# Moving one gate load of the second chunk from the head of the input transfers to behind the seventh weight piece

## The chip, the cores and the metric

The kernel runs on one core of a Trainium2 chip. The metric is the time of one execution in microseconds on the device, and the median over several executions is what two versions are compared by. The engines named below are TensorE (PE, its weight loads PEld), VectorE (DVE), ScalarE (ACT), GpSimd (POOL) and SyncE (SP), which computes nothing here and only issues transfers.

## The reference

Two layers follow each other. The first is a gated linear attention over 4 batches, 8 heads, 768 steps and a head dimension of 48:

```
f = 1.0 / (1.0 + np.exp(-f_logit))
for t in range(S):
    state = f[:, :, t, :, None] * state + np.einsum('bhd,bhe->bhde', k[:, :, t], v[:, :, t])
    y[:, :, t] = np.einsum('bhd,bhde->bhe', q[:, :, t], state)
```

Its output, 3072 rows of 384 (8 heads times 48), goes through four dense experts of width 1024, whose outputs are added with the normalized weights of each row:

```
p = domain_probs / (domain_probs.sum(-1, keepdims=True) + 1e-09)
for e in range(E):
    h = np.maximum(x @ w1[e], 0.0)
    out += p[:, e:e + 1] * (h @ w2[e])
```

All tensors come and go as 32-bit floats. The matrix products run in bf16.

## The kernel before, in words

The 768 steps are cut into 6 chunks of 128. Inside a chunk the recurrence becomes matrix products. For each batch the gate logits `f` go through an exponential (line 260) and a logarithm (264) on ACT, a triangular product on TensorE sums them along the steps (268), two exponentials of the sums (288) scale `q` and `k` (296), both are transposed (305 on TensorE in the first chunks, 309 by DMA later), and then come the masked products (320, 324), the output (331, 335), the state (341, 348, 355), and the transposed output `xT` (360 on TensorE, 313 by DMA), which the experts read. The four batches of a chunk make 512 rows. For them the first expert layer takes 24 matmuls per expert (364: 8 blocks of 128 columns, 3 blocks of the inner dimension), its results pass the relu on ACT (375) or DVE (373), and the second layer (379) takes 32 matmuls, whose results are weighted and added on DVE (386) or ACT (388).

Chunk 0 must run its attention before any expert work can start. From there on the attention of the next chunk runs beside the expert work of the current one. While TensorE waits in chunk 0, idle matmuls on a tile `busy` (614) keep it occupied; the planner says how many.

The weights of the experts are loaded once, by DMAs that GpSimd issues (239) and that cast to bf16. There are 11 pieces, numbered from 0: pieces 0 and 1 are the two halves of the first layer of expert 0, 2 and 3 those of expert 1, 4 and 5 the halves of the second layer of expert 0, then whole layers follow: 6 is the first layer of expert 2, 7 the second of expert 1, 8 the first of expert 3, 9 the second of expert 2, 10 the second of expert 3. Pieces 0 to 5 write 384 KB each and the rest 768 KB. Piece 0 waits for the last `q` of chunk 0 (line 241), so that the inputs of chunk 0 go first; piece 10 waits for `k` of chunk 1 (243).

The inputs are loaded by DMAs that SyncE issues (232), in the order of its queue. Chunk 0 has one load of 192 KB per tensor and batch. Of chunk 1, the gate logits of batch 0 come next, alone; those of batch 1 wait for piece 8 (`w_gate`), and behind them stand `k`, `q` and `v` of batches 0 and 1 and all of batches 2 and 3, in loads of 384 KB. The first exponential of chunk 1 reads the logits of batches 0 and 1 in one instruction, so it needs both loads. A queue runs in order: a load that waits holds everything behind it on SyncE.

No order is written out by hand. `Plan.run` simulates the engines with a list of operations, each with a cost per engine, a priority and its dependences, and gives out the buffers. Each step takes the ready operation of the lowest priority number, and the kernel emits the instructions in that order. The two halves of a copy or a relu may therefore land on ACT or DVE, depending on the planned times. A load is an operation of the planned engine "DMA"; `cost=0.1` for the moved load is a planned cost, not a measured one. `after(x, y)` makes the DMA x wait on the chip until the DMA y has landed.

Of the kernel before, what the change touches and what calls it, by code (L numbers as in the profile page):

```python
# [102 lines left out]
def kernel(  # L103
# [85 lines left out]
    ins = {}  # L189
# [10 lines left out]
    def tl(kind, *key):  # L200

        if (kind, key) not in tiles:
            room = kind if kind in rooms else "ps_m" if kind in ("hp", "op", "pp") else "ps_t"
            slot = P.slot[(room, kind) + key if room.startswith("ps_") else (room,) + key]
            if room in ("gp", "qk", "e"):
                tiles[kind, key] = pads[room, slot]
            else:
                shape, dt = shapes[kind]
                pool = ps if room.startswith("ps_") else wk
                tiles[kind, key] = pool.tile(shape, dt, name=f"{room}{slot}")  # L210
        return tiles[kind, key]

    def after(later, earlier):
        tc.add_manual_dep(later.ins, earlier.ins.name,
                          mybir.DependencyInfo(mybir.DependencyClass.Sync, mybir.DependencyReason.DATA),
                          reason="order of transfers")
# [4 lines left out]
    def hh(b, n=1):  # L221
        return slice((b % 2) * H, (b % 2 + n) * H)
# [8 lines left out]
    def load(c, nm, b, n):  # L231
        ins[c, nm, b] = nc.sync.dma_start(out=tl(nm, c, b // 2)[:, hh(b, n), :],  # L232
                                          in_=srcs[nm][c, :, b * H:(b + n) * H, :])
        if (c, nm, b) == (1, "f", 1):
            after(ins[c, nm, b], ins["w", w_gate])

    def load_w(i, e, which, ks, cols):
        w, r = (w1_sb, w1_r) if which == 1 else (w2_sb, w2_r)
        ins["w", i] = nc.gpsimd.dma_start(out=w[:, e, ks, cols], in_=r[e][:, ks, cols])  # L239
        if i == 0:  # L240
            after(ins["w", 0], ins[0, "q", B - 1])
        if i == w_last:
            after(ins["w", i], ins[1, "k", 0])
# [154 lines left out]
    def add_load(c, nm, b, n, prio, deps=(), cost=None):  # L398
        op = P.add(f"ld {nm}{c}.{b}", {"DMA": cost or (1.05 if c else 1.1) * n}, lambda e: load(c, nm, b, n), prio,
                   deps=deps, takes=[(nm, c, b // 2)], lag=2.0)  # L400
        for i in range(n):
            ld[c, nm, b + i] = op
        return op

    for i, x in enumerate("f0 k0 q0 f1 k1 q1 f2 f3 k2 q2 v0 k3 q3 v1 v2 v3".split()):
        add_load(0, x[0], int(x[1]), 1, -1000 + i)
    add_load(1, "f", 0, 1, -980, cost=0.1)

    every = slice(0, None)
    pieces = [(e, 1, every, slice(i * F // 2, (i + 1) * F // 2)) for e in range(2) for i in range(2)]  # L410
# [2 lines left out]
    w_last, w_gate = len(pieces) - 1, len(pieces) - 3  # L413
    wd = {}
    for i, (e, which, ks, cols) in enumerate(pieces):
        if i == w_last:
            for x in ((1, "f", 1, 1), (1, "k", 0, 2), (1, "q", 0, 2), (1, "v", 0, 2)):
                add_load(*x, -430 + len(ld), deps=wd[3, 1])
        iss = P.add(f"w issue {i}", {"POOL": 0.8}, lambda _, i=i, x=(e, which, ks, cols): load_w(i, *x),
                    -500 + i, deps=[ld[0, "q", B - 1]] + ([ld[1, "k", 0]] if i == w_last else []))  # L420
        op = P.add(f"w {i}", {"DMA": 2.25 if i < 6 else 4.5}, lambda _: None, -400 if i == w_last else -460 + i, deps=[iss], lag=1.5)
        wd[e, which] = wd.get((e, which), []) + [op]
# [226 lines left out]
```

## Time and profile before

| what | value |
|---|---|
| median of 5 runs | 299.07 us (298.53 to 299.54) |
| the profiled execution | 299.54 us |
| its span, first to last instruction | 297.7 us |
| granted TensorE clock | 1.0 of full speed |
| busy: PE, ACT, DVE, POOL | 287.3, 176.3, 125.8, 106.4 us |
| moved by DMA | 36.82 MB, mean 124 GB/s |

The profiled execution is the slowest of the five shown. Times inside it are counted from the first instruction; the remaining 1.84 us lie around the span. A name such as "PE ps_m L364" means the engine, the tile it writes and the line of the kernel. "SPq" is SyncE's queue, and the length of a row there is the time that the issue took, waits included, not the transfer. The time from an issue to the landing of its data is a number of its own. Some matmul records are missing from the trace, a few per cent, which looks like short gaps.

### The profile page before, as it was taken

How to read it: one execution, taken by the hardware profiler on the slowest of the kernel's cores; microseconds unless marked ns; L12 is line 12 of the kernel's file. 1: busy time of each engine (PE TensorE's matmuls, PEld its weight loads, DVE VectorE, ACT ScalarE, POOL GpSimd, SP SyncE). 2: the span in 40 equal slices, each digit the busy share in tenths (PEclk: the TensorE clock that was granted, in tenths of full speed). 3: DMA queues.
4: the chain of work that ended last, by engine and by line, in shares of the span. 5: the costliest groups of instructions: out<-in, count | busy, mean ns of one | idle time of the engine just before them, and what ended most of it. 6: DMA issues, size and time to landing. Idle time of an engine off the chain costs nothing.

```text
span 297.7 us, 5544 instructions
## 1 busy us (share of the span) xinstructions
PE 287.3 (96%) x2132; PEld 170.6 (57%) x2160; DVE 125.8 (42%) x247; ACT 176.3 (59%) x325; POOL 106.4 (36%) x179
## 2 busy tenths in 40 slices
PE   6969999999999999999999999999999999999995
PEld 2547555567777776455565555555555555555553
DVE  6757002685674583036375444332533322201223
ACT  5866664847675686777465574545465544465440
POOL 5387301329488159235448463234220000000000
PEclk9999999999999999999999999999999999999999
DMA  7999999976979969995989952102432100200003
GB/s 155 214 190 206 207 207 213 203 139 169 185 154 196 210 138 188 201 222 93 208 156 208 186 110 36 29 0 62 115 64 39 26 2 26 79 2 0 0 0 108
DMA packets 136462, 36.82 MB, mean 124 GB/s; under 512 B 126812, under 2 KB 135644, under 8 KB 136436
## 3 DMA queue, kind: packets, MB, share of 16 engines
q1 hardware_dynamic: 129348, 30.14, 50.7%
q0 software_dynamic: 7088, 6.33, 13.6%
q8 instruction: 17, 0.28, 0.4%
q14 instruction: 9, 0.07, 0.1%
HBM read 31.51 MB, written 4.72 MB: 122 GB/s over the span
## 4 chain that ended last, share of the span: by engine, by line
PE 91%; DMA 3%; SPq 3%; issue 1%; DVE 1%
PE ps_m L379 42%; PE ps_m L364 41%; SPq L232 3%; DMA w_sb<-in_moe_w_dram 2%; PE ps_t L320 2%; PE ps_t L335 1%; PE ps_t L331 1%; DMA q<-in_q_dram 1%; PE ps_t L341 1%; PE ps_t L268 1%; PE ps_t L305 0%; SPq L247 0%; DVE h L373 0%; DVE o L386 0%; PE ps_t L360 0%
## 5 line engine op out<-in xcount | busy, mean ns | idle before, releaser
L375 ACT ACTIVATE h<-ps_m 128x512 bf16<-128x512 f32 (+1 forms) x192 | 102.5, 538 | 93.7 <-PE ps_m L364 89.9
L364 PE MATMUL ps_m<-xT,w_sb 128*128 128x512 bf16 (+1 forms) x670 | 150.1, 341 | 3.5 <-DMA w_sb<-in_moe_w_dram 2.0
L379 PE MATMUL ps_m<-w_sb,h 128*128 128x384 bf16 (+1 forms) x776 | 151.6, 324 | 0.2
L379 PEld LDWEIGHTS <-h 128*128 128x128 bf16 x776 | 75.1, 98 | 58.6
L386 DVE SCALAR_TENSOR_TENSOR o<-ps_m,pn,o 128x384 f32<-128x384 f32 (+1 forms) x73 | 44.7, 612 | 110.6 <-PE ps_m L379 104.3
L364 PEld LDWEIGHTS <-w_sb 128*128 128x128 bf16 x696 | 65.5, 98 | 45.1 <-DMA w_sb<-in_moe_w_dram 2.7
L296 POOL TENSOR_TENSOR qk<-q,e 128x384 bf16<-128x384 f32 x19 | 22.9, 1208 | 36.6 <-ACT e L288 34.3
L324 DVE TENSOR_TENSOR AT<-ps_t,mask 128x512 bf16<-128x512 f32 x48 | 29.9, 683 | 5.5 <-PE ps_t L320 5.4
L355 POOL TENSOR_TENSOR Sf<-Sf,egs 48x192 f32<-48x192 f32 x40 | 20.2, 504 | 32.5 <-DVE Sf L348 30.4
L288 ACT ACTIVATE e<-ps_t 128x384 f32<-128x384 f32 x48 | 26.7, 666 | 4.0 <-PE ps_t L268 2.9
L373 DVE TENSOR_SCALAR h<-ps_m 128x256 bf16<-128x256 f32 (+1 forms) x40 | 20.0, 510 | 20.0 <-PE ps_m L364 17.8
L296 POOL TENSOR_TENSOR qk<-k,e 128x384 bf16<-128x384 f32 x20 | 20.4, 1024 | 8.8 <-ACT e L288 4.3
L348 DVE TENSOR_TENSOR Sf<-Sf,ps_t 48x192 f32<-48x192 f32 x40 | 14.0, 351 | 11.0 <-PE ps_t L341 9.7
L239 POOL DMA_DIRECT2D w_sb<-in_moe_w_dram x11 | 9.0, 824 | 20.2 <-DMA k<-in_k_dram 16.6
L356 POOL CAST sb<-Sf 48x192 bf16<-48x192 f32 x40 | 13.6, 340 | 2.6
L388 ACT ACTIVATE o<-ps_m,pn 128x384 f32<-128x384 f32 x22 | 12.8, 581 | 2.8 <-PE ps_m L379 1.8
L293 POOL DMA_DIRECT2D egs<-e x16 | 9.0, 565 | 10.4 <-ACT e L288 10.4
L614 PE MATMUL ps_m<-busy 128*128 128x512 bf16 x32 | 10.5, 427 | 1.6 <-DVE busy L144 1.5
L226 ACT CAST yb<-ps_t 128x384 bf16<-128x384 f32 (+1 forms) x16 | 7.6, 472 | 7.5 <-PE ps_t L335 7.3
L335 PE MATMUL ps_t<-vb,AT 128*128 128x48 bf16 x192 | 11.5, 185 | 0.4 <-DVE vb L228 0.4
L260 ACT ACTIVATE ex<-f 128x768 f32<-128x768 f32 (+1 forms) x14 | 10.5, 748 | 2.1 <-DMA f<-in_f_logit_dram 2.0
L335 PEld LDWEIGHTS <-AT 128*128 128x128 bf16 x192 | 9.9, 97 | 2.1 <-DVE vb L228 0.5
(54 smaller groups left out, 122.5 us busy)
## 6 DMA issues: line engine op xcount, KB each, us to landing
out_dram<-o SPq DMA_DIRECT2D x23, 192.0 KB, 2.0
w_sb<-in_moe_w_dram POOLq DMA_DIRECT2D x5, 768.0 KB, 18.5
k<-in_k_dram SPq DMA_DIRECT2D x10, 384.0 KB, 4.8
q<-in_q_dram SPq DMA_DIRECT2D x10, 384.0 KB, 5.1
v<-in_v_dram SPq DMA_DIRECT2D x10, 384.0 KB, 5.2
f<-in_f_logit_dram SPq DMA_DIRECT2D x9, 384.0 KB, 4.7
w_sb<-in_moe_w_dram POOLq DMA_DIRECT2D x6, 384.0 KB, 9.5
f<-in_f_logit_dram SPq DMA_DIRECT2D x6, 192.0 KB, 4.0
```

What stands on the lines that cost most here:

```text
L288: nc.scalar.activation(out=o, in_=i, func=AF.Exp, scale=1.0 if j else -1.0)
L296: engines[eng].tensor_tensor(out=tl("qk", c, b)[:, j, :, 0:D].rearrange("t (i r) d -> t i r d", r=2), in0=tl("qk"[j], c, b // 2)[:, hh(b), ...
L324: nc.vector.tensor_tensor(out=tl("AT", c, b)[:, r].rearrange("s i t -> s (i t)"), in0=tl("A", c, b, r).rearrange("s i t -> s (i t)"), in1= ...
L335: nc.tensor.matmul(out=y[:, h * D:(h + 1) * D], lhsT=AT[:, r, i, :], rhs=vb[:, h, :], start=(c == 0), stop=True, skip_group_check=True)
L348: nc.vector.tensor_tensor(out=Sf[rows, b], in0=Sf[rows, b], in1=KV[rows, :, r, :], op=ALU.add)
L355: nc.gpsimd.tensor_tensor(out=Sf[rows, b], in0=Sf[rows, b], in1=eg, op=ALU.mult)
L356: nc.gpsimd.tensor_copy(out=nb[rows, b, :, r * D:(r + 1) * D], in_=Sf[rows, b])
L364: nc.tensor.matmul(out=tl("hp", c, e, fc, n0)[:, n0:n1], lhsT=w1_sb[:, e, kk, fc * 128:(fc + 1) * 128], rhs=tl("xT", c)[:, kk, n0:n1], sta ...
L373: nc.vector.tensor_relu(out=dst, in_=src)
L375: nc.scalar.activation(out=dst, in_=src, func=AF.Relu)
L379: nc.tensor.matmul(out=tl("op", c, e, nt, part)[:, cols], lhsT=tl("h", c, e, half_of(c, nt * T))[:, fc, nt * T:(nt + 1) * T], rhs=w2_sb[:, ...
L386: nc.vector.scalar_tensor_tensor(out=o, in0=op, scalar=pe, in1=o, op0=ALU.mult, op1=ALU.add)
```

## The change

The load of the gate logits of chunk 1, batch 0 (192 KB) is no longer planned among the inputs of chunk 0. It is added where the pieces of weights are planned, ahead of the issue of piece 7, with a dependence on piece 6 (`wd[2, 1]`, the first layer of expert 2) and a priority between the two, and on the chip it waits until piece 6 has landed.

```
     def load(c, nm, b, n):
         ins[c, nm, b] = nc.sync.dma_start(out=tl(nm, c, b // 2)[:, hh(b, n), :],
                                           in_=srcs[nm][c, :, b * H:(b + n) * H, :])
+        if (c, nm, b) == (1, "f", 0):
+            after(ins[c, nm, b], ins["w", 6])
         if (c, nm, b) == (1, "f", 1):
             after(ins[c, nm, b], ins["w", w_gate])
...
         add_load(0, x[0], int(x[1]), 1, -1000 + i)
-    add_load(1, "f", 0, 1, -980, cost=0.1)
...
     for i, (e, which, ks, cols) in enumerate(pieces):
+        if i == 7:
+            add_load(1, "f", 0, 1, -454.5, deps=wd[2, 1], cost=0.1)
         if i == w_last:
```

SyncE's transfers keep their order, and so do GpSimd's instructions. Because the planner's times change, a few copies and relus change between ACT and DVE around 26 and 66 us, and on TensorE the two products of line 268 for batches 2 and 3 of chunk 1 come ahead of the transposes of line 360 for batch 1 instead of behind them.

More of the change, by code (lines that the diff above doesn't have):

```diff
@@ L233, in load @@
                                           in_=srcs[nm][c, :, b * H:(b + n) * H, :])
+        if (c, nm, b) == (1, "f", 0):
+            after(ins[c, nm, b], ins["w", 6])
         if (c, nm, b) == (1, "f", 1):
@@ L406 @@
         add_load(0, x[0], int(x[1]), 1, -1000 + i)
-    add_load(1, "f", 0, 1, -980, cost=0.1)
     every = slice(0, None)
@@ L415 @@
     for i, (e, which, ks, cols) in enumerate(pieces):
+        if i == 7:
+            add_load(1, "f", 0, 1, -454.5, deps=wd[2, 1], cost=0.1)
         if i == w_last:
```

## The prediction

> **What bounds the kernel now.** I read the page's busy times and slices first, then TensorE's waits, then the chain that ended last around its only long stop, then the transfers there, one by one. Pieces of weights are numbered from 0, as in the code, so the seventh is piece 6; chunks and batches count from 0 too.
>
> The page's parts 1 and 2:
>
> ```profile
> PE 287.3 (96%) x2132; PEld 170.6 (57%) x2160; DVE 125.8 (42%) x247; ACT 176.3 (59%) x325; POOL 106.4 (36%) x179
> PE   6969999999999999999999999999999999999995
> PEclk9999999999999999999999999999999999999999
> DMA  7999999976979969995989952102432100200003
> ```
>
> TensorE is busy from the third slice to the last, at the full clock. The waits of TensorE over the whole span (a row: who waited for whom, total us, times, longest):
>
> ```profile
> PE ps_m L364 <- DMA w_sb<-in_moe_w_dram: 2.0, 1, 2.0
> PE ps_m L614 <- DVE busy L144: 1.5, 1, 1.5
> PE ps_t L268 <- ACT gp L264: 1.0, 2, 0.7
> ...
> PE ps_m L364 <- DVE psm L255: 0.3, 1, 0.3
> ```
>
> And of its weight loads, from 15 to 30 us:
>
> ```profile
> PEld L364 <- DMA w_sb<-in_moe_w_dram: 2.7, 2, 2.1
> ```
>
> The same question from 30 us to the end gives no row at all: after 24.14 us TensorE never waits (single gaps of 0.05 us are missing records). So whatever moves the start of the dense part moves the end, unless a new wait appears. The start is set by weights, as the chain from 9 to 30 us says (start, length, what):
>
> ```profile
> 11.47 3.53 DMA q<-in_q_dram
> 14.99 0.30 issue
> 15.29 6.83 DMA w_sb<-in_moe_w_dram
> 22.12 0.05 issue
> 22.17 0.84 PE ps_m L364 x6
> ```
>
> Piece 0 of the weights is issued at 15.29, lands at 22.12, and the first matmul of L364 starts at 22.17. The second row of the weight loads is 0.6 us for piece 1, which lands at 24.09; the matmul at 24.14 starts 0.05 us later (the list of waits puts it down to DVE L255, which ended then too, but L364 doesn't read psm). Both stops are the weights' pace. SyncE's queue in order of time shows who is ahead of them:
>
> ```profile
> 12.09 2.92 SPq L232 DMA_DIRECT2D v<-in_v_dram  x3
> 15.05 28.37 SPq L232 DMA_DIRECT2D f<-in_f_logit_dram  x2
> 43.46 0.58 SPq L232 DMA_DIRECT2D k<-in_k_dram  x1
> ```
>
> The first of the two f rows is the load that moves: issued at 15.05, 0.24 us before piece 0, landing 6.35 us later, at 21.40. The stretches show what the DMA engines did (columns: stretch, length, busy of PE, PEld, DVE, ACT, POOL, clock, DMA share, GB/s):
>
> ```profile
> 17.00:18.00 1.00, 0.90 (x18) 0.57 (x16) 0.24 (x2) 0.86 (x2) 1.00 (x2) 1.00 1.12 203
> 18.00:19.00 1.00, 0.74 (x13) 0.48 (x13) 1.00 (x3) 0.59 (x3) 1.00 (x2) 1.00 1.05 156
> 21.00:22.00 1.00, 0.00 (x0) 0.00 (x0) 0.00 (x0) 0.00 (x0) 0.70 (x1) 1.00 1.25 207
> ```
>
> They were full all the time, first with SyncE's packets (from 15.3 to 17.5 us not one packet of the weights' queue is recorded; its first starts at 17.54), then with weights. The last 0.197 MB of SyncE's bytes, the size of this load, start from 17.1 us on, all but 0.02 MB of it before 18.3.
>
> **The change part by part.**
>
> *The load leaves its place.* It is 128x384 floats, 196,608 bytes. After the f that lands at 9.16, loads of this size land at 10.33, 11.00, 12.09, 13.01 and, past the small one for the probabilities, at 14.15, 14.99 and 15.95: seven in 6.79 us, 0.97 each. Weights run at the same rate: pieces 0 to 5 land 1.93 us apart ((31.79 - 22.12) / 5) for 393,216 bytes written, so 196,608 bytes are 0.97 again. If weights simply move up by these bytes, pieces 0 and 1 land 0.97 earlier. From below: the move can be worth less if piece 0 is then late by its own path from issue to first packet. Its 6.83 us are 1.93 of transfer and 4.90 of other time. The nearest row is piece 10, 8.09 us for twice the bytes (3.87), so 4.22 of other time, also behind SyncE's packets; that would allow 4.90 - 4.22 = 0.68. A transfer of 2 KB from the same queue (the egs rows, median 3.3 us, least 2.5) would allow more than 0.97. So 0.68 to 0.97, and 0 as the end if piece 0's first packet at 17.54 had nothing to do with SyncE's. I take 0.87: nearer to the bytes, because the engines were full before and after the handover. Above 0.97 there is only the handover itself: 156 and 150 GB/s between 18 and 20 us against 205 after are 0.10 MB, 0.5 us, which I expect to move with it; if it vanished, the gain were near 1.5.
>
> [...]
>
> *TensorE before the weights.* The last attention matmul of chunk 0 ends at 20.18 (19.82 + 0.36); rows of xT that the first L364 needs are copied by 20.28. Weights at 22.12 - 0.87 = 21.25 are still later, so the whole 0.87 is TensorE's. Then L364 at 24.14 goes to 23.27 with piece 1.
>
> *The new wait.* SyncE's order does not change: the load still comes right after the v loads, and now waits for piece 6 (landed 35.50, then about 34.6). Queued behind it is only f of batch 1, which already waits for piece 8 until 43.04, then k, q, v of chunk 1. GpSimd's queue gains no wait. Cost nothing; the cover is the 8 us between pieces 6 and 8.
>
> *The load in its new place.* It now meets pieces 7 to 9, so these keep their landings (39.31, 43.04, 46.97), while TensorE comes 0.87 earlier. First uses: piece 7 at 42.38, 8 at 49.52, 9 at 51.46, 10 (which waits for k of chunk 1) at 61.77 against 57.85. The least margin is 42.38 - 39.31 = 3.07, then 2.20. Pieces 4 (30.70 against 29.80), 5 (33.30 against 31.79) and 6 (39.14 against 35.50) move up with the rest. Cost nothing. The load's reader, the 768-wide exponential on ACT at 52.15, becomes due at 51.3; f of batch 1, which it needs as well and which still goes at piece 8, landed at 47.80.
>
> *What the planner does with it.* The planner's clock starts the weights 0.1 us earlier, and some copies change engine. Around 26 us one relu of 0.42 us goes from DVE to ACT and one back, with one pair of L348 ahead of it: by the rows there each of the four result buffers is free 0.3 us or more before its next matmul. Around 66 us a copy of yb and one of xT (0.48 us each on ACT) go to DVE, and the two L268 matmuls of batches 2 and 3 stand before the transposes L360 of batch 1 instead of after them. In the old times: their gate is ready on ACT at 65.8, the buffers at 65.5 and 66.1, L268 comes at 66.35; yb is ready at 66.1, L360 due at 66.68; xT is done at 68.1, L364 due at 68.80. Cost nothing, with 0.26 us the smallest margin.
>
> *Later.* One margin is narrow: at 89.29 L364 reads an xT transposed by DMA that landed at 88.98. That queue is led by POOL and DVE steps that follow TensorE, so it should move too; I take 0.05 off for it and the copies.
>
> Sum: 0.87 - 0.05 = 0.82. The profiled execution took 299.54 (span 297.7, 1.84 around it): 299.54 - 0.82 = 298.72. That execution is the slowest of five; the median is 299.07, so 298.25.
>
> **The rivals.**
>
> *Piece 0 starts no earlier* (the change does nothing at its place). For it: the first weight packet comes 1.33 us after the issue ended at 16.21, and the rate climbs slowly to 20 us. Against: SyncE's packets hold every engine until 17.5. Between no gain and 0.6: 298.5 to 299.1.
>
> *The gain is given back at 89 us.* If the transfers of chunk 2, with DMA at nine tenths between 75 and 100 us, keep their times, xT lands at 88.98 while L364 comes at 88.47: 0.51 lost, 0.31 left: 298.8. Against: the queue's head, f at 70.07, waits for an output store, which waits for TensorE.
>
> *Slower: the gate logits starve behind weights.* An f load issued at 49.16 beside piece 10 took 10.13 us, and the k issued after it held SyncE for 5.24; between 52.7 and 55 us the weights' queue moved 0.44 MB and SyncE's next to nothing. In its new place the load has pieces 7 to 9 beside it. If it, and f of batch 1 behind it, land after 51.3, ACT stops at the exponential with the relu of L375 behind, and TensorE runs out of result buffers; beyond 52.2 the gain is gone, and at 53.0 the kernel is 0.2% slower, 299.7. That asks for a landing 5.2 us later than 47.80. Against: piece 9 ends at 46.97, and SyncE's packets flowed at once then.
>
> **How the numbers follow.** About 0.2% (0.6 us) is what a measurement can tell from no change. The forecast's own case (a gain of 0.6 to 1.0, 298.0 to 298.5) has 0.60; piece 0 no earlier 0.20; given back 0.12; starving 0.08. A shift of medians between sessions (the five runs span 1.0 us) puts a little of the second case above. Faster 0.61, same 0.29, slower 0.10. The range: from 297.7 (0.97 and part of the handover's 0.5) to 299.4 (no gain, and the spread of the runs); the likeliest case alone 298.0 to 298.5.
>
> **What would show it.** Right: SyncE issues this f at about 34.6 us, the first L364 starts near 21.3 and the fifth group of three near 23.3, TensorE has no wait after that, and pieces 7 to 9 land where they did, within a few tenths. Wrong: piece 0 still lands at 22; or it lands early and rows of L364, L379 or L320 with a wait for DMA or ACT appear at 40 to 53 or at 88 us.

## The result and the profile after

The changed kernel takes 298.19 us (median of 30 runs, 297.68 to 299.34). The kernel before, run beside it, takes 299.0 us (52 runs, 298.36 to 299.96). The ratio is 0.9978, with a 95% interval from 0.9971 to 0.9985: faster by 0.15 to 0.29%, or about 0.65 us. The medians lie 0.81 us apart. The forecast was 298.25.

The profiled execution of the changed kernel took 298.97 us with a span of 297.3, so it is one of its slower ones. Compared with the profiled execution before (299.54 and 297.7) only about 0.5 us are gone. The profile shows a gain at the start and two stops behind it that take part of it back. Two lines were added above most of the code, so line 364 of before is 366 now, 379 is 381, 239 is 241 and 260 is 262.

The page's busy times and slices:

```profile
PE 287.9 (97%) x2132; PEld 170.8 (57%) x2160; DVE 127.3 (43%) x249; ACT 175.5 (59%) x323; POOL 105.6 (36%) x179
...
PE   6889999999999999999999999999999999999995
...
PEclk9999999999999999999999999999999999999999
```

The third slice of TensorE, from 14.9 to 22.3 us, was 6 and is 8: there is less idle time ahead of the dense part, and it is as dense as before after it. The waits of TensorE over the whole span (who waited for whom, total us, times, longest):

```profile
PE ps_m L366 <- DMA w_sb<-in_moe_w_dram: 0.8, 2, 0.6
PE ps_m L381 <- DMA w_sb<-in_moe_w_dram: 0.5, 1, 0.5
```

The wait for the first weights fell from 2.0 us to 0.6, and that for piece 1 is now listed by its right name. The second row is new. TensorE in order of time shows where the rows belong (start, length, engine, line, operation, and in brackets the idle time before it):

```profile
21.18 1.16 PE L366 MATMUL ps_m<-xT,w_sb 128*128 128x256 bf16 x9 [0.60 <-DMA w_sb<-in_moe_w_dram]
...
23.08 0.50 PE L366 MATMUL ps_m<-xT,w_sb 128*128 128x256 bf16 x3 [0.24 <-DMA w_sb<-in_moe_w_dram]
...
61.37 1.46 PE L381 MATMUL ps_m<-w_sb,h 128*128 128x384 bf16 x8 [0.46 <-DMA w_sb<-in_moe_w_dram]
```

Piece 0 starts the expert work at 21.18 instead of 22.17, and the matmul behind piece 1 starts at 23.08 instead of 24.14. That is 1.06 us won. At 61.37 TensorE stands still for piece 10, which landed at 61.33 against 57.85 before. The stretches around the handover from the inputs to the weights, columns as in the prediction:

```profile
17.00:18.00 1.00, 0.93 (x7) 0.61 (x8) 1.00 (x3) 1.00 (x3) 1.00 (x2) 1.00 0.61 72
18.00:19.00 1.00, 1.00 (x26) 0.75 (x23) 0.43 (x2) 0.86 (x3) 1.00 (x2) 1.00 1.13 172
19.00:20.00 1.00, 0.98 (x13) 0.46 (x10) 1.00 (x2) 1.00 (x3) 1.00 (x2) 1.00 1.21 192
```

The inputs now end about 1 us sooner, and the first weight packet starts at 16.89 instead of 17.54. The hole between the two has moved with them and is not smaller: against 205 GB/s these three us lack 0.18 MB, where before they lacked 0.11.

A smaller stop, too short for the list of waits, comes with piece 5 near 32 us (TensorE in order of time again):

```profile
30.94 1.46 PE L366 MATMUL ps_m<-xT,w_sb 128*128 128x512 bf16 x6
32.38 2.11 PE L381 MATMUL ps_m<-w_sb,h 128*128 128x384 bf16 x12
```

The six matmuls of L366 start 0.216 us apart, so the L381 behind them was due at 32.24. It starts at 32.38, 0.04 us after piece 5 has landed (32.34).

The chain that ended last used to go through TensorE from 22 us on. Now it reaches TensorE only at 61.37 us, through transfers (start, length, what):

```profile
21.67 22.55 DMA w_sb<-in_moe_w_dram
44.66 6.71 DMA k<-in_k_dram
51.91 9.43 DMA w_sb<-in_moe_w_dram
61.37 1.46 PE ps_m L381 x8
```

Piece 8 lands at 44.23 (43.04 before), which releases the second f load and then `k` of chunk 1, whose landing releases piece 10. SyncE's queue shows the moved load at its new place (start and length of the issue, waits included):

```profile
36.07 8.54 SPq L232 DMA_DIRECT2D f<-in_f_logit_dram  x2
44.66 0.57 SPq L232 DMA_DIRECT2D k<-in_k_dram  x1
```

It is issued when piece 6 has landed, and lands 11.48 us later, at 47.55. Its first packet starts only at 39.61. At its old place it took 6.35. The queues in the stretch from 39.5 to 45.5 us (packets, MB, share of 16 engines):

```profile
q0 software_dynamic: 967, 0.95, 93.9%
q1 hardware_dynamic: 953, 0.18, 27.6%
```

Here q0 carries the weights and q1 SyncE's transfers. They get the same number of packets, but the rows of `f` are 192 bytes each and those of the weights about 1 KB. So the load moves 0.03 MB per us, and the weights fall to 0.16 MB per us. Before, from 39.5 to 44.5, they had 1.02 MB in 5 us, 0.20 per us.

The sum of the two profiled executions: 1.06 won at piece 1; 0.14 lost at piece 5 (the L381 behind it starts at 32.38 instead of 33.30, only 0.92 earlier); 0.46 lost at piece 10. That leaves 0.46, and the spans differ by 0.48 (297.74 and 297.26 before rounding). The 0.14 are not the moved load's doing: piece 5 landed at 32.34, 0.55 later than before, and the load was issued only at 36.07. In the other profiles of the changed kernel piece 5 landed at 31.66 and 31.23; why it was late here stays open.

### The profile page after: what moved, and what is told of

Read it like the earlier page. It is cut to its first block, busy times and chain, and to the rows that moved or that the text cites. A ratio compares the mean times of both kernels' runs of the same rounds, so it can differ in the third digit from the quotient of the medians.

```text
span 297.3 us, 5545 instructions
## 1 busy us (share of the span) xinstructions
PE 287.9 (97%) x2132; PEld 170.8 (57%) x2160; DVE 127.3 (43%) x249; ACT 175.5 (59%) x323; POOL 105.6 (36%) x179
## 4 chain that ended last, share of the span: by engine, by line
PE 78%; DMA 14%; SPq 4%; POOL 2%; issue 1%; DVE 0%; POOLq 0%
PE ps_m L381 37%; PE ps_m L366 35%; DMA w_sb<-in_moe_w_dram 11%; SPq L232 3%; DMA k<-in_k_dram 2%; POOL w_sb L241 2%; PE ps_t L322 2%; PE ps_t L337 1%; PE ps_t L333 1%; DMA q<-in_q_dram 1%; PE ps_t L270 1%; PE ps_t L343 1%; SPq L249 0%; DVE o L388 0%; PE ps_t L362 0%
## 5 line engine op out<-in xcount | busy, mean ns | idle before, releaser
L381 PE MATMUL ps_m<-w_sb,h 128*128 128x384 bf16 (+1 forms) x776 | 151.5, 324 | 0.7 <-DMA w_sb<-in_moe_w_dram 0.5
L366 PE MATMUL ps_m<-xT,w_sb 128*128 128x512 bf16 (+1 forms) x670 | 150.1, 341 | 2.0 <-DMA w_sb<-in_moe_w_dram 0.8
L381 PEld LDWEIGHTS <-h 128*128 128x128 bf16 x776 | 75.2, 98 | 59.2 <-issue 0.7
L366 PEld LDWEIGHTS <-w_sb 128*128 128x128 bf16 x696 | 65.5, 98 | 43.6 <-DMA w_sb<-in_moe_w_dram 1.2
L228 POOL CAST vb<-v 128x384 bf16<-128x384 f32 x18 | 9.9, 568 | 3.8 <-PE ps_m L366 2.2
```

The costliest lines, as they stand in the source:

```text
L366: nc.tensor.matmul(out=tl("hp", c, e, fc, n0)[:, n0:n1], lhsT=w1_sb[:, e, kk, fc * 128:(fc + 1) * 128], rhs=tl("xT", c)[:, kk, n0:n1], sta ...
L381: nc.tensor.matmul(out=tl("op", c, e, nt, part)[:, cols], lhsT=tl("h", c, e, half_of(c, nt * T))[:, fc, nt * T:(nt + 1) * T], rhs=w2_sb[:, ...
```

## The experiments

Four theories were tried. A: the start gains about 1 us, and the load at its new place holds piece 10 back, which costs time. B: the new place costs nothing in the usual execution. C: the wait on piece 6 makes the whole gain, because the span is the start of the matmul behind piece 1 plus a constant. D: the planner's new order of copies has a part in it.

**The changed kernel again.** No edit.

> The changed kernel once more, for a second profile. Theory A (the start gains about 1.0 us, and the moved load, which trickled for 11.5 us beside pieces 7 to 9, holds piece 10 back so that TensorE waits for it near 61 us): first L366 again at 21.0 to 21.3 us against 22.17, piece 8 lands after 43.5, piece 9 after 48, piece 10 after 60, and a wait of L381 at 61 us between 0 and 0.6 us; time 0.6 to 0.9 below the kernel before. Theory B (the wait at 61 us was an accident of that one execution; the new place costs nothing): pieces 8 to 10 land within 0.5 us of the kernel before (43.0, 47.0, 57.9) and no wait at 61.

Measured: 298.17 us, ratio 0.9979 to the kernel before (0.9964 to 0.9994). Piece 1's matmul starts at 22.96. Piece 8 lands at 43.55, piece 9 at 48.48, piece 10 at 60.11. TensorE needs piece 10 37.63 us after that matmul (61.77 - 24.14 in the profile before), so at 60.59: it is there 0.48 us ahead, and no wait at 61 us appears. Pieces 8 to 10 are late again, as A says, but the slack, 3.92 us before, just holds. So the wait in the first profile is not in every execution.

**The load with piece 8 instead of piece 6.**

```diff
-            after(ins[c, nm, b], ins["w", 6])
+            after(ins[c, nm, b], ins["w", w_gate])
```

> The changed kernel with one word changed: the moved load waits for piece 8 instead of piece 6, so it goes together with the load of batch 1; the planned order of all engines is the same. Theory A: no transfer of SyncE runs beside pieces 7 and 8, which land near 39 and 42.5, piece 9 near 46.5, piece 10 no later than 59.5, no wait of L381 at 61 us, and 0.1 to 0.5 us faster than the changed kernel. Theory B: the same time as the changed kernel within 0.1.

Measured: 298.33 us, ratio 0.9977 (0.9964 to 0.9991). Pieces 7, 8 and 9 land at 38.41, 42.10 and 45.96, as A says for a load that no longer runs beside them. To leave out how late the whole row of pieces was, count from the landing of piece 6: piece 9 comes 11.47 us after it before the change, 13.10, 13.03 and 13.10 in three profiles of the changed kernel, and 11.46 here. So the load costs the weights beside it 1.6 us. The slack of piece 10 (59.40 against 60.44 needed) is 1.04 us, and there is no wait. But the kernel is not faster than the changed one. The cost of the new place is real in the landings, and it does not show in the median.

**The planner's order without the wait.** The two added lines in `load` are left out; the load stays where the change planned it.

```diff
-        if (c, nm, b) == (1, "f", 0):
-            after(ins[c, nm, b], ins["w", 6])
```

> The changed kernel without the wait on piece 6: SyncE issues the load at about 15 us, as before the change, while the planned order of copies, relus and of L270 and L362 is the changed one. Both theories: the time of the kernel before within 0.2 us (298.8 to 299.2), first L366 near 22.1. A rival, that the planner's new order made part of the gain: 0.3 us or more below the kernel before.

> The plan without the wait, a second time, because the first was 0.37 us below the kernel before where nothing was expected. Theory C: the time of the kernel before within 0.2 us, the matmul behind piece 1 at 23.8 to 24.2. Rival D: 0.3 to 0.4 below the kernel before, with the matmul behind piece 1 at 24.0 and the end less than 273.4 us after it.

Measured: 298.57 us, ratio 0.9991 (0.9982 to 0.9999), and the second time 299.66 beside a kernel before of 299.79, ratio 0.9997 (0.9979 to 1.0016). The first profile has piece 1's matmul at 23.92 and ends 273.57 us after it, as the kernel before does (297.74 - 24.14 = 273.60). So no gain from the order shows behind 24 us. The second profile can't be read this way: it is the slowest of its twelve executions (301.31), with a stretch at half the clock from 23.17 us on. The first median, 0.37 below the kernel before, is more than was expected, and the second, 0.13 below, is not; what of the first is real stays open.

The first profile also corrects a reading. Here L364 starts at 21.38 and not near 22.1 as expected, almost as early as in the changed kernel, and then stands for piece 1:

```profile
PE ps_m L364 <- DMA w_sb<-in_moe_w_dram: 2.4, 2, 1.5
```

The two stops together last 2.4 us. It is piece 1 that sets the pace, not piece 0.

**The wait without the planner's order.** The kernel before keeps its order on every engine; only the load itself goes behind piece 6.

```diff
     def load(c, nm, b, n):
+        if (c, nm, b) == (1, "f", 0):
+            tl(nm, c, 0)
+            return
+        if (c, nm, b) == (1, "f", 1):
+            first = nc.sync.dma_start(out=tl(nm, c, 0)[:, hh(0, 1), :], in_=srcs[nm][c, :, 0:H, :])
+            after(first, ins["w", 6])
```

> The kernel before with its own planned order on every engine, and only the load of the first gate logits held on the chip until piece 6 has landed. Theory C (the span is the start of the matmul that waits for piece 1, plus 273.6 us, plus what later waits add; the wait on piece 6 makes the whole gain): first L364 at 20.9 to 21.2, the one behind piece 1 at 22.8 to 23.1, time that of the changed kernel within 0.15 us (298.0 to 298.35). Rival D (the planner's new order makes 0.3 of it): 298.4 to 298.7.

Measured: 299.15 us beside 299.79 for the kernel before, ratio 0.9976 (0.9957 to 0.9996). The times of this chip are some 0.8 us higher, so the absolute times expected were missed; the difference is that of the changed kernel. The profile, TensorE in order of time:

```profile
21.68 1.16 PE L370 MATMUL ps_m<-xT,w_sb 128*128 128x256 bf16 x9 [0.70 <-DMA w_sb<-in_moe_w_dram]
...
23.62 0.50 PE L370 MATMUL ps_m<-xT,w_sb 128*128 128x256 bf16 x3 [0.30 <-DMA w_sb<-in_moe_w_dram]
```

It ends 273.61 us after the second of these. On the same chip, with the load in its old place, piece 1 landed at 24.68 (the second run of the order alone), here at 23.58. Of these 1.10 us, 0.27 are an earlier issue of piece 0 (15.78 and 15.51), which the load does not set; counted from that issue it is 8.90 against 8.07, so 0.83. The order of the kernel before with the wait has the ratio of the changed kernel, so the wait is enough for the gain. C holds, D is not shown.

**An additional load in the old place.** The changed kernel, with 192 KB loaded where the moved load was; nothing reads them.

```diff
+        if (c, nm, b) == (0, "v", 3):
+            nc.sync.dma_start(out=idle, in_=srcs["f"][1, :, 0:H, :])
         if (c, nm, b) == (1, "f", 0):
```

> The changed kernel with an additional load of 192 KB, which nobody reads, in the place that the moved load left. It measures the early place by itself: the difference to the changed kernel is what a load there costs. Theory A: first L366 near 22.1 and the whole 1.0 us back at the start; at the end a little less, because TensorE then comes later to piece 10 and has less or nothing to wait for at 61 us: 0.5 to 1.0 above the changed kernel. Theory B: 0.8 to 1.0 above it. A rival, that piece 0 is late by its own path: no difference at the start.

Measured: 299.1 us, 0.93 above the changed kernel in the same comparison, ratio 1.0005 to the kernel before (0.9991 to 1.0018). So a load in this place costs the whole gain. The expectation on its place was wrong: the first L366 (L369 in this file) starts at 20.64, earlier than in the changed kernel. The unread load landed at 23.38, after 8.62 us, overtaken by piece 0. The price is paid at piece 1, whose matmul starts at 23.60 after a stop of 1.30.

**A second load at the new place.** The changed kernel, with another 192 KB that nothing reads, right behind the moved load.

```diff
             after(ins[c, nm, b], ins["w", 6])
+            nc.sync.dma_start(out=idle, in_=srcs["f"][1, :, 0:H, :])
```

> The changed kernel with a second load of 192 KB, which nobody reads, behind the moved one, so beside pieces 7 to 9 too. It doubles the suspected cost of the new place. Theory A (such a load delays piece 10 by 1.3 us or more, of which 0.5 us of slack are left): piece 10 lands after 61.3, L381 waits for it at 61 us for 0.5 to 1.5 us, 0.4 to 1.5 us slower than the changed kernel. Theory B (the new place costs nothing): within 0.2 of the changed kernel.

> The changed kernel with the second, unread load beside pieces 7 to 9 once more, for a second profile, since its median was 1.1 us above that of the changed kernel's order with the wait alone while its profiled execution shows no wait at 61 us (piece 10 landed 0.26 us before it was needed). Theory A (piece 10 is late in most executions): a wait of L381 near 61 us of 0.5 us or more, with the clock at 1.0 throughout. Rival E (TensorE's clock: a stretch at half clock near 22 us, as in two other profiles, cost the time): no wait at 61 us, and a granted clock below 1.0 between 20 and 28 us.

Measured: 300.25 us beside 299.79 before (1.0003, 0.9985 to 1.0021), and 299.69 beside 299.05 (1.0007, 0.9988 to 1.0026). In the same two comparisons the wait alone had 299.15 and the changed kernel, run a third time, 298.54; so the medians are 1.10 and 1.15 higher. By the ratios (0.9976 and 0.9979 there) it is about 0.8 us, and the intervals overlap a little; these runs spread over 1.9 and 3.6 us. The first profile has piece 10 0.26 us ahead of TensorE, the second has it late:

```profile
PE ps_m L383 <- DMA w_sb<-in_moe_w_dram: 1.9, 1, 1.9
```

The same profile in stretches (length, busy of PE, PEld, DVE, ACT, POOL, granted clock, DMA share, GB/s):

```profile
60.00:63.00 3.00, 1.17 (x20) 0.71 (x19) 3.00 (x6) 0.38 (x1) 0.00 (x0) 1.00 1.27 209
63.00:66.00 3.00, 2.96 (x19) 1.72 (x19) 0.99 (x3) 0.00 (x0) 0.00 (x0) 0.53 1.23 223
66.00:69.00 3.00, 3.00 (x40) 2.24 (x38) 2.20 (x7) 2.07 (x3) 1.65 (x4) 0.90 0.55 132
```

Piece 10 landed at 63.00. TensorE stood for 1.87 us, and then ran at half the clock for a while. This supports A: the new place spends piece 10's slack, and a second load of the same kind overdraws it. Rival E's half clock is there too, but at 63 us and behind the wait. The records do not show E as the cause of the medians: an execution with a stretch at half clock has a mean granted clock of 0.994, as this profile does, while all twelve executions of the first comparison and ten of the eleven of the second have 0.998 or more. (An execution whose clock was not recorded counts as 1.0; the first profile is such a one.) Whether most executions wait, two profiles can't say.

**The load behind piece 3.** It then runs beside pieces 4 to 7.

```diff
-            after(ins[c, nm, b], ins["w", 6])
+            after(ins[c, nm, b], ins["w", 3])
```

> The changed kernel with the moved load waiting for piece 3 instead of piece 6, so that it runs beside pieces 4 to 7. Theory A (beside weights it takes about half of the packets for some 6 us and pushes the pieces back by about 1.5 us): the start as in the changed kernel, but pieces 5 and 6 about 1 us later than there; piece 5 has 0.1 to 0.5 us of slack, so L381 waits for it near 32 us for 0.5 to 1.2 us, and the kernel is 0.4 to 1.2 us slower than the changed one. Theory B: within 0.2 of the changed kernel.

Measured: 299.23 us beside 299.79 before, ratio 0.9973 (0.9953 to 0.9992), the gain of the changed kernel. The load took 11.7 us to land (27.72 to 39.40), and its packets came late, the first at 31.49: piece 5 landed at 31.52, not moved, and piece 7 9.11 us after it, against 7.52 before. So the 1.6 us fell on pieces 6 and 7, which had 3 us of slack, and not on piece 5. A named the wrong victim, and the time did not change. Its profile has half the clock from 22 us on, so a stop near 32 us can't be compared.

**A version that might beat both: piece 0 behind the last k.**

```diff
-            after(ins["w", 0], ins[0, "q", B - 1])
+            after(ins["w", 0], ins[0, "k", B - 1])
```

> The changed kernel with piece 0 waiting for the last k of chunk 0 (landed 14.21) instead of the last q (14.96). A version that may beat both, since piece 1 sets the start: pieces 0 and 1 are issued 0.75 us earlier and land 0.3 to 0.75 earlier, if the last v loads, which then share the engines with them, do not hold chunk 0's attention: 0.2 to 0.7 us faster than the changed kernel. If they do (v of batch 3 landed 18.48, used at once), the end of chunk 0's attention moves back by as much and the gain is 0 or a loss of up to 0.5.

> The changed kernel a third time, beside the version above. Theory C: its span is the start of the matmul behind piece 1 plus 273.5 to 273.7 us, plus the length of any wait near 32 and 61 us, plus about 1.2 us if the clock is halved in a stretch near 22 us; piece 10 lands less than 1.2 us before or just after TensorE needs it.

Measured: 298.88 us, ratio 1.0002 (0.9976 to 1.0029), against 298.54 and 0.9979 (0.9963 to 0.9995) for the changed kernel beside it. Piece 0 is issued at 14.46 instead of 15.19, and yet lands at 21.22 instead of 21.31, piece 1 at 23.10 instead of 23.20. The first weight packet starts at 17.04, against 16.82 in the changed kernel beside it: the engines were full with inputs (195 to 223 GB/s from 14 to 17 us), so the earlier issue only waits longer. Three of the twelve executions show a clock of 0.993 or 0.994; the other nine have a median of 298.46. Either way it is no better. The changed kernel's third profile ends 273.58 us after the matmul behind piece 1 (296.83 - 23.25), with piece 10 at 60.16, 0.72 ahead, as C said.

C over the profiles, from the start of piece 1's matmul to the end of the span, with the waits near 32 and 61 us taken off. The three profiles with a stretch at half clock are left out.

| kernel | piece 1's matmul | to the end | slack of piece 10 |
|---|---|---|---|
| before | 24.14 | 273.60 | 3.92 |
| changed | 23.08 | 273.58 | none, 0.46 late |
| changed, again | 22.96 | 273.59 | 0.48 |
| changed, third | 23.25 | 273.58 | 0.72 |
| load with piece 8 | 22.81 | 273.57 | 1.04 |
| order without the wait | 23.92 | 273.57 | 2.45 |
| wait without the order | 23.62 | 273.61 | 0.36 |
| extra load, old place | 23.60 | 273.50 | 0.31 |
| second load, new place, first profile | 23.36 | 273.52 | 0.26 |
| piece 0 behind the last k | 23.15 | 273.57 | 1.75 |

## Why the prediction was right

*What bounds the kernel.* Right. TensorE is dense behind piece 1, and the end follows that one start within 0.1 us in every row above.

*The load leaves its place: 0.87.* The mechanism was right, and so was the size, as far as the runs can tell. The two profiles give 1.06, but single profiles scatter, and the one before is an execution 0.54 us above the median of its kernel. A steadier measure is the time from the issue of piece 0 to the landing of piece 1. With the load in its old place it is 8.80 us (before), 8.63 and 8.90 (the order without the wait). In eight profiles without it there and with the same release of piece 0 it is 7.59 to 8.12, on average 7.86. Between the averages lie 0.92 us; with the unread load in the old place it was 8.31, only 0.45 more. So 0.87 fits, and the bounds of 0.68 and 0.97 can't be told from it. As the prediction expected, the slow handover from the inputs to the weights only moved and did not shrink.

*The rival "piece 0 starts no earlier"* fell: 21.18 against 22.17, and the additional load in the old place brings the loss back. But the runs also show that piece 0 was not the gate to watch. With a load in the old place it landed at 21.34 and 20.60 in two of four profiles, about as early as in the changed kernel (21.03 to 21.31) or earlier, and piece 1 still came 0.4 to 1.0 us later than there.

*The load in its new place: "cost nothing".* This step failed in the first profile, and the two others of the same kernel bear it out only by a narrow margin. It said that pieces 7 to 9 keep their landings. They landed 0.65, 1.19 and 2.19 us later, and piece 10, through `k` of chunk 1, 3.48 us later; in the others 2.26 and 2.31. The margins were read correctly, but as if only TensorE moved towards them. Of the 3.92 us of piece 10, TensorE's earlier start takes 1.1. Not all of the rest is the load's: with the load in its old place, and only the order changed, piece 10 landed at 59.10, already 1.25 later than in the profile before, so the 57.85 there lies low. In the first profile 0.46 us were lost, in the two others nothing. Of the prediction's own signs, the early start came as said (21.18 and 23.08 for 21.3 and 23.3); "no wait after that" failed in the first profile, and "pieces 7 to 9 land where they did" in all three.

*The rival "the gate logits starve behind weights"* had the mechanism and the wrong victim. The load took 11.48 us. But the exponential on ACT never waited: both loads had landed by 49.84, and it started at 51.23. Those who came late were the weights and `k` behind it.

*What the planner does: cost nothing.* Right as far as shown.

*The narrow margin at 89 us: 0.05.* Not needed. That xT landed at 88.38 and was read at 88.82, 0.44 us of slack against 0.31, since the chain that leads there moved with TensorE.

The forecast of 0.82 met the difference of the medians, 0.81. The mechanism earned it in the main, but not to the hundredth: the ratio says 0.65 us (0.45 to 0.87), and the slack of piece 10, which the prediction did not count as spent, happened to last in two of three profiles. How many executions give part of the gain back was not measured.

## What to carry to other kernels

Where one engine is dense to the end, find the last wait ahead of the dense part, here the second weight piece and not the first, and take bytes out of the queue ahead of it; here they were worth about their transfer time (0.92 us between the averages, 0.97 us between the landings of such loads). Then follow the moved transfer down every chain it joins, here through the landing of piece 8 and of `k` to the issue of piece 10, and count what it takes from each slack, not only from the transfer's own reader. A change that is free today can have used up the room for the next one: a second load at the same place cost about 1.1 us between the medians, 0.8 by the ratios.

## What the runs showed of the hardware

From 39.5 to 45.5 us in the changed kernel the load of `f`, in rows of 192 bytes, and the full weights queue beside it got about as many packets each: 953 of 0.18 MB against 967 of 0.95 MB. The total fell from 203 and 205 GB/s (before, 40 to 44 us) to 191 and 184. And the load started late: its first packet came 3.5 to 3.8 us after its issue in the three profiles of the changed kernel (36.07 to 39.61, 35.46 to 39.00, 34.95 to 38.53) and in that with the load behind piece 3 (27.72 to 31.49).

In three profiles TensorE's granted clock dropped to half (0.50) for a stretch, each time after a stop of less than 2 us: after stops of 1.70 us (the order alone, second time) and 1.67 us (the load behind piece 3) at the start of the weights, and after that of 1.87 us for piece 10. The stretches of the second of them, the load behind piece 3:

```profile
20.00:22.00 2.00, 0.33 (x10) 0.22 (x8) 0.29 (x1) 0.79 (x2) 2.00 (x3) 1.00 1.20 197
22.00:24.00 2.00, 2.00 (x11) 1.41 (x12) 0.42 (x1) 0.38 (x1) 0.84 (x2) 0.50 1.24 204
24.00:26.00 2.00, 2.00 (x20) 1.63 (x19) 1.37 (x6) 1.32 (x4) 0.92 (x1) 0.65 1.24 204
```

From 22.00 the clock is 0.50, and over the two stretches it lacks (1 - 0.50 + 1 - 0.65) x 2 = 1.70 us of full clock. The other two profiles lack 1.72 us (0.79, 0.50 and 0.85 in the three stretches of 2 us from 22 to 28 us) and 1.71 us (0.53 and 0.90 in those of 3 us from 63 to 69 us). At 0.50 that is an estimated 3.4 us of half clock each time. In the profile with the wait for piece 10, the end comes 1.56 us later than the constant of the table and the wait explain (300.49 - 23.48 - 273.58 - 1.87). The kernel before had a stop of 1.99 us and kept its clock (1.00 from 20 to 26 us), so the length of the stop does not decide alone. What else decides was not shown; no run here placed a stop on purpose.

As far as the clock was recorded, the gain of the change is not of this kind: the changed kernel run again and the kernel before beside it have a mean clock of 0.998 or more in all 12 and 35 executions, and their medians still lie 0.77 us apart.
